# Products of zeros behind three steps of the first triangular solve, and two transposes tied to their written place

## The chip, the core and the metric

The kernel runs on one core of a Trainium2 chip. The metric is the device time of one execution in microseconds (us); the time before is the median of three runs. The engines are called PE (TensorE; its weight loads are listed apart, as PEld), DVE (VectorE), ACT (ScalarE), POOL (GpSimd) and SP (SyncE, whose queue issues the loads and stores).

## The reference

Two parts follow each other. The first is a linear attention with the delta rule over 4 batches x 8 heads, 768 steps and head size 48, in f32; the second is one wide layer on its result, with 3072 tokens, 384 inputs and 2048 hidden columns.

```python
k_n = k / (np.linalg.norm(k, axis=-1, keepdims=True) + 1e-06)
for t in range(S):
    y[:, :, t] = q_t @ state
    v_old = k_t @ state
    state = state + beta_t * outer(k_t, v_t - v_old)
h = x @ w_in
g = h * tanh(log1p(exp(h)))
out = g @ w_out
```

## The kernel before

**Stages.** The 768 steps are cut into 12 chunks of 64, and every two chunks form a group. Inside a chunk the steps depend on each other through a triangular system, so the kernel inverts triangles first. `early(g)` (line 253) does it for a group: DVE transposes the keys of each of the two chunks (`kt`, line 264), PE forms the products of keys with keys (`pg`, line 283), DVE takes the masked part (`d`, line 286), transposes it (`gt`, line 294), scales it, and then solves by forward substitution. A step j of the solve is two DVE instructions, a multiply into the tile `pr` (line 336) and an addition into `gt` (line 338). For the first two groups the triangles are cut into halves of 16 rows, so that j runs from 1 to 14; `merge` puts the halves together with small PE products (`ma`, line 375, and `mb`, line 386). The tile `pr` has one buffer: each step's `pr` takes the place of the one before. Behind the last step DVE scales the result and transposes it twice (`tt`, line 345, and `tu`, line 349); `ma` reads `tu`.

After that a chunk goes through `s_a`, `s_b`, `s_gq`, `s_z` and `s_y` (small products, all recorded under line 433, told apart by their tiles `ta`, `tb`, `gq`, `pz`, `py` and `ps`), and its 256 rows of results are transposed (`xt`) for the wide layer. `moe(n)` does that layer for a chunk: `g1(fp)` forms `h` (line 575) and a chain of ACT and DVE steps from it (lines 588 to 595, of which 589, 593 and 595 are DVE's), `g2(fp)` sums into `acc` (line 610).

**Conversions.** The weights come as 64-bit floats. `convert` (line 206) turns 28 parts of them, one by one, into two f32r halves: one ACT step (line 219), four DVE steps (lines 221 to 227), a product with the identity (`loi` or `loo`, line 238, f32, and line 241), and two ACT copies. They are laid between the other work over about the first 160 us.

**Order of work.** Every piece of work is a generator that is put on a plan with times (`put`); `run` pops them in order of planned time, and `defer` puts a follow-up a little later. Plan times are the author's estimates, not device time. `us(t)` turns a position in chunks into a plan time: `us(0)` is 76, `us(1)` is 140. What is popped is written into the program in that order. Up to plan time 90 the framework orders all engines anew, by a simulated timeline with the written order as priority, and may let an instruction whose inputs seem ready float ahead; from 90 on PE keeps the order in which it was written, and the other engines are still ordered by the framework. `order(a, b)` and `tc.keep_in_program_order(a)` add an edge without a wait: `a` stays behind `b`, or behind the instruction of the same engine that was written last before it. For groups from the third on the transposes of the keys are already tied in this way (line 267). For the second group they are written at plan times 85 and 92.

**Loads.** The keys of chunks 2 and 3 have source tiles of their own, loaded early; SP's queue issues all loads in a chain (`load`, line 169).

**Products of zeros.** `keep_warm(n)` (line 631) issues n bf16 products of 128 x 128 zeros with 128 x 512 zeros into the tile `warm`, 14 + 3 + 6 of them near the start of the plan.

Of the kernel before, what the change touches and what calls it, by code (L numbers as in the profile page):

```python
# [35 lines left out]
def kernel(  # L36
# [22 lines left out]
    nc = tc.nc  # L59


    TN = dict(fg=2, pl=range(0, 28), po=8, pg=(), db=1, fixed=((90.,()),(1e9,('PE',))),
              d0=["k0",1,"k1","b",3,"q",3,"v","x",4,"k2",4,"k3",13],
              us=[76., 140., 192., 242.],
              warm=[(0.5,14),(16.5,3),(18.,6)],
# [3 lines left out]
              cv=[(10.5,0),(12.8,1),(16,1.6),(23,2),(36,3),(74,13),(120,27.2),(123,28)],  # L69
              e1=[85,86,87.2,92,93,94.2,107,111], s1=(0.62,0.98), f1=0.985, m2=(1.0,1.02,1.03,1.05), m3=(1.18,1.2,1.22,1.24),  # L70
              prep1=52., prep2=0.4, c0=0.12, ab=(0.04,0.08), c1=(0.3,0.45,0.68,0.82), c2=(0.2,0.38,0.57,0.75), cc=(0.05,0.28,0.5,0.72),
              u1g=(1.085,1.12,1.45,1.3), ug=(0.81,0.93,1.56), g2=(-3.2,-2.75,-2.7,-2.69,-2.67,-2.64,-2.631), gg=(-4.05,-3.85,-3.692,-3.691,-2.85,-2.692,-2.691), tx=1.1, sg=-1.5, clk=1e9, mg=(-1.39, -1.36, -1.33, -1.30))
    FG = TN['fg']
    B, H, S, D = q.shape
    NT, DM = out.shape
# [1 line left out]
    P = 128  # L77
# [88 lines left out]

    loaded = []

    def load(dst, src):

        m = nc.sync.dma_start(out=dst, in_=src)  # L171
        if loaded and len(loaded) < TN.get('lo', 150):
            order(m, loaded[-1])
        loaded.append(m)

    def load_src(dst, src, n):
        for hh in range(2):
            for ch in range(2):
                w = 32 if ch == 0 else D - 32
                for tb in range(2):  # L180
                    t0 = C * n + 32 * tb
                    r0 = 64 * (1 - hh) + 32 * ch
                    load(dst[r0:r0 + 32, :, tb, :w], src[hh, t0:t0 + 32, :, 32 * ch:32 * ch + w])


    def load_w(parts):
# [66 lines left out]
    def early(g):  # L253
        dt = ap.tile([P, 2, NP, 32], F32, tag="d", name=f"d{g}", bufs=TN["db"])
        split = g < FG
        dts[g] = dt
        for t2 in range(2):
            n = 2 * g + t2
            ks = srcs.get((g, t2), ksrc)
            if g > 1 and t2 == 0:  # L260
                load_src(ks, kk, n)
                yield
            kt = kts[n] = ap.tile([P, NP, 2, 32], F32, tag="kt", name=f"kt{n}", bufs=3)
            m = nc.vector.transpose(kt.rearrange("p a b c -> p (a b c)"), ks.rearrange("p a b c -> p (a b c)"))
            m
            if g > 1:
                tc.keep_in_program_order(m)
                if t2 == 0:
                    load_src(ks, kk, n + 1)
            yield  # L270
            at = ats[n] = ap.tile([P, NP, 32], F32, tag="at", name=f"at{n}", bufs=3)
            for h8 in range(2):
                tensor(1.05)
                ps = pa.tile([P, 8, C], F32, tag="at", name=f"pg{n}_{h8}")
                for p8 in range(8):
                    p = 8 * h8 + p8

                    for c in range(2):
                        for hh in range(2):
                            r = slice(64 - 64 * hh, 128 - 64 * hh)  # L280
                            r0 = 64 * hh + 32 * c
                            mv = kt[r, p] if c else kt[r, p, 0:1, :].broadcast_to([64, 2, 32])
                            nc.tensor.matmul(ps[r0:r0 + 32, p8, :], kt[r, p, c, :], mv, start=True, stop=True)

                def out(t2=t2, ps=ps, at=at, pr=slice(8 * h8, 8 * h8 + 8)):
                    nc.vector.tensor_tensor(out=dt[:, t2, pr, :], in0=ps[:, :, 32:],
                                            in1=bcast_mid(lmask, 8), op=ALU.mult)
                    nc.scalar.copy(out=at[:, pr, :], in_=ps[:, :, 0:32])

                defer(1.2, out)  # L290
                yield
        gr = ap.tile([P, 33, 32], F32, tag="gt", name=f"gt{g}", bufs=1)
        gt = gr[:, :32]
        nc.vector.transpose(gt, dt.rearrange("p a b f -> p f (a b)"))
        gf = gt.rearrange("p a b -> p (a b)")
        if split:

            nc.gpsimd.memset(gt[:, 16:, 0:16], 0.0)
            nc.gpsimd.memset(dt[:, :, :, 0:16], 0.0)

        ss = ap.tile([P, 32], F32, tag="ss", name=f"ss{g}", bufs=1)
        nc.vector.tensor_scalar(ss, gf[:, ::33], 1e-30, None, op0=ALU.max)
        y = ap.tile([P, 32], F32, tag="y", name=f"y{g}", bufs=1)
        nc.scalar.activation(y, ss, AF.Ln, scale=0.25)
        nc.scalar.activation(y, y, AF.Exp, scale=0.5)
        yield
        rc = ap.tile([P, 32], F32, tag="rc", name=f"rc{g}", bufs=1)
        nc.vector.reciprocal(rc, y)
        nc.vector.scalar_tensor_tensor(ss, ss, 0.25, rc, op0=ALU.mult, op1=ALU.mult)
        nc.vector.scalar_tensor_tensor(ss, ss, 1e-6, y, op0=ALU.add, op1=ALU.add)  # L310
        nc.vector.reciprocal(rc, ss)
        nb = ap.tile([P, 32], F32, tag="nb", name=f"nb{g}", bufs=1)
        nc.vector.scalar_tensor_tensor(nb, rc, -1.0, rc, op0=ALU.mult, op1=ALU.mult)
        nc.vector.tensor_tensor(out=nb, in0=nb, in1=betaT[:, g, :], op=ALU.mult)

        nb_, sz = (2, 16) if split else (1, 32)
        blk = gr.rearrange("p a b -> p (a b)")[:, :nb_ * (1056 // 2)] if split else gf
        blk = blk.rearrange("p (x r) -> p x r", x=nb_)[:, :, :32 * sz].rearrange("p x (i j) -> p x i j", j=32)
        blk = blk[:, :, :, :sz]
        by_col = [P, nb_, sz, sz]  # L320
        nc.vector.tensor_tensor(
            out=blk, in0=blk, in1=nb.rearrange("p (x j) -> p x j", x=nb_).unsqueeze(2).broadcast_to(by_col),
            op=ALU.mult)
        nc.gpsimd.memset(gf[:, ::33], 1.0)
        bp = ap.tile([P, 32], F32, tag="bp", name=f"bp{g}")
        nc.vector.tensor_scalar(bp, nb, -1.0, None, op0=ALU.mult)
        ne = nes[g] = ap.tile([P, 32], F32, tag="ne", name=f"ne{g}")
        nc.vector.transpose(ne, ss)  # L328
        yield
        for j in range(1, sz - 1):  # L330
            m = sz - 1 - j
            pr = ap.tile([P, 512], F32, tag="prod", name=f"pr{g}_{j}", bufs=1)
            pv = pr[:, :nb_ * m * j].rearrange("p (x a b) -> p x a b", x=nb_, b=j)
            below, xj = blk[:, :, j + 1:, :j], blk[:, :, j:j + 1, :j].broadcast_to([P, nb_, m, j])
            nj = blk[:, :, j + 1:, j:j + 1].broadcast_to([P, nb_, m, j])
            nc.vector.tensor_tensor(out=pv, in0=nj, in1=xj, op=ALU.mult)  # L336
            yield
            nc.vector.tensor_tensor(out=below, in0=below, in1=pv, op=ALU.add)  # L338
            yield
        nc.vector.tensor_tensor(  # L340
            out=blk, in0=blk, in1=bp.rearrange("p (x i) -> p x i", x=nb_).unsqueeze(3).broadcast_to(by_col),
            op=ALU.mult)
        if not split:
            yield
        nc.vector.transpose(tt2[:, :, :, 32:].rearrange("p a b i -> p i (a b)"), gt)
        tn = tns[g] = ap.tile([P, 2, NP, 32], F32, tag="tn", name=f"tn{g}", bufs=1)
        if split:
            tu = tus[g] = ap.tile([P, 2, NP, 16], F32, tag="prod", name=f"tu{g}", bufs=1)
            nc.vector.transpose(tu.rearrange("p a b j -> p j (a b)"),
                                      gt[:, :, 0:16].rearrange("p i j -> p j i"))  # L350
            ym = yms[g] = ap.tile([P, 33, 32], F32, tag="gt", name=f"ym{g}", bufs=1)
            nc.gpsimd.memset(ym[:, :32, 16:], 0.0)
        else:
            nc.vector.transpose(tn.rearrange("p a b j -> p j (a b)"), gt.rearrange("p i j -> p j i"))
            for t2 in range(2):
                move_diagonal(t2)
        yield
# [270 lines left out]
    zb = zero.bitcast(BF16)  # L628
    warm = ph.tile([P, 512], F32, tag="h", name="warm")

    def keep_warm(n):
        tensor(0.4 * n)
        for _ in range(n):
            nc.tensor.matmul(warm, zb[:, 0:P], zb[:, :512], start=True, stop=True)

    ys, xs = {}, {}

# [22 lines left out]
    def load_beta():  # L660
        for c in range(2):
            for hh in range(2):
                for t2 in range(2):
                    r0 = 64 * hh + 32 * c + 16 * t2
                    load(betaT[r0:r0 + 16], bt[hh, c, t2])

    todo = list(parts)

    def loads(order):
        for x in order:  # L670
# [11 lines left out]
                    load_k(0, h)  # L682
            else:
                m = int(x[1])
                load_src(srcs[m // 2, m % 2], kk, m)

    took = {s_a: 1.2, s_b: 1.2, s_gq: 1.1, s_z: 1.1, s_y: 1.9}

# [35 lines left out]
    for i, p in enumerate(parts):  # L724
        ts = [when(i + j / 4 + 0.1) for j in range(4)]
        end = ts[3] + 0.75
        put(convert(*p), ts[0] - 0.75, *ts, end, end + 0.8, end + 1.4, end + 2.4)

    units = [moe(n) for n in range(NS)]
    todo1 = [(n, fp) for n in range(NS) for fp in range(NFP)]  # L730
# [89 lines left out]
```

## Time and profile before

| | |
|---|---|
| time, median of 3 runs | 704.14 us (702.71 to 704.75) |
| the profiled execution, its own time | 702.13 us |
| its span, first to last instruction | 700.3 us |
| granted clock, mean | 0.944 |
| PE busy | 633.6 us, 90% of the span |
| DVE busy | 478.4 us, 68% |
| ACT busy | 440.0 us, 63% |
| the key transposes of chunks 2 and 3 (line 264) | start at 45.26 and 76.11 us, 1.25 us each |
| first `ma` behind the first solve | 58.58 us |

A row of the order of time reads: start, duration (of the first to the last, where several are merged), engine, line, operation, written tile <- read tiles, shape, count, and in brackets how long the engine had been idle before it and what ended that. "issue" there means that nothing in the profile explains the wait. A row of a table by stretches gives for each engine its busy time and number of instructions, then the granted PE clock as a share of full speed, the mean busy share of the DMA engines, and GB/s.

### The profile page before, as it was taken

How to read it: one execution, taken by the hardware profiler on the slowest of the kernel's cores; microseconds unless marked ns; L12 is line 12 of the kernel's file. 1: busy time of each engine (PE TensorE's matmuls, PEld its weight loads, DVE VectorE, ACT ScalarE, POOL GpSimd, SP SyncE). 2: the span in 40 equal slices, each digit the busy share in tenths (PEclk: the TensorE clock that was granted, in tenths of full speed). 3: DMA queues.
4: the chain of work that ended last, by engine and by line, in shares of the span. 5: the costliest groups of instructions: out<-in, count | busy, mean ns of one | idle time of the engine just before them, and what ended most of it. 6: DMA issues, size and time to landing. Idle time of an engine off the chain costs nothing.

```text
span 700.3 us, 23223 instructions
## 1 busy us (share of the span) xinstructions
PE 633.6 (90%) x10163; PEld 582.5 (83%) x10163; DVE 478.4 (68%) x1048; ACT 440.0 (63%) x821; POOL 48.8 (7%) x84
## 2 busy tenths in 40 slices
PE   6543899889979899999999999999999999999993
PEld 3313777679879799999999999999999999999993
DVE  4794278996449975589974799856899645443440
ACT  1350368776535766856758766668566687777771
POOL 5000000101000001010010000010100100000000
PEclk9575589999989999999999999999999999999998
DMA  5999230113131232222212312321121111000000
GB/s 81 223 244 348 40 61 12 22 15 59 27 63 26 42 59 39 41 52 35 46 37 42 63 25 39 66 37 30 31 35 47 28 21 36 13 22 3 12 12 24
DMA packets 160214, 37.79 MB, mean 54 GB/s; under 512 B 153456, under 2 KB 156528, under 8 KB 160112
## 3 DMA queue, kind: packets, MB, share of 16 engines
q1 hardware_dynamic: 160112, 36.30, 25.4%
q8 instruction: 80, 1.31, 0.7%
q14 instruction: 22, 0.18, 0.1%
HBM read 31.56 MB, written 4.72 MB: 52 GB/s over the span
## 4 chain that ended last, share of the span: by engine, by line
PE 44%; DVE 26%; ACT 13%; SPq 7%; issue 6%; DMA 3%; DVEq 0%; ACTq 0%
PE h L575 15%; PE acc L610 15%; SPq L171 7%; DVE e L593 4%; PE gq L433 3%; ACT e L591 3%; DVE g L595 3%; DVE pr L336 3%; DVE gt L338 3%; ACT e L590 2%; PE py L433 2%; ACT e L592 2%; DVE e L589 2%; DVE xx L480 2%; DVE xx L421 2%
## 5 line engine op out<-in xcount | busy, mean ns | idle before, releaser
L575 PE MATMUL h<-x,wi 128*128 128x256 f32 x1728 | 227.0, 285 | 4.3 <-DVE e L593 3.6
L575 PEld LDWEIGHTS h<-x,wi 128*128 128x128 f32 x1728 | 214.4, 188 | 10.5 <-DVE e L593 2.9
L610 PE MATMUL acc<-wo,g 128*128 128x384 f32 x1152 | 221.1, 341 | 0.0
L610 PEld LDWEIGHTS acc<-wo,g 128*128 128x128 f32 x1152 | 198.4, 188 | 3.2
L593 DVE SCALAR_TENSOR_TENSOR e<-e,h 128x512 f32<-128x512 f32 x96 | 65.8, 685 | 97.1 <-ACT e L592 93.8
L590 ACT ACTIVATE e<-e 128x512 f32<-128x512 f32 x96 | 60.6, 631 | 74.6 <-DVE e L589 74.1
L594 ACT CAST g<-e 128x512 fp32r<-128x512 f32 x96 | 59.5, 619 | 41.3 <-DVE e L593 40.8
L595 DVE TENSOR_TENSOR g<-e,g 128x512 fp32r<-128x512 f32 x96 | 65.1, 678 | 20.6 <-ACT g L594 19.4
L588 ACT ACTIVATE e<-h 128x512 f32<-128x512 f32 x96 | 57.1, 595 | 28.5 <-PE h L575 27.6
L591 ACT ACTIVATE e<-e 128x512 f32<-128x512 f32 x96 | 60.5, 631 | 2.6
L592 ACT ACTIVATE e<-e 128x512 f32<-128x512 f32 x96 | 60.6, 632 | 2.4
L589 DVE TENSOR_SCALAR e<-e 128x512 f32<-128x512 f32 x96 | 40.8, 425 | 25.1 <-ACT e L588 24.8
L338 DVE TENSOR_TENSOR gt<-gt,pr 128x84 f32<-128x84 f32 (+14 forms) x148 | 46.0, 311 | 3.2
L336 DVE TENSOR_TENSOR pr<-gt 128x84 f32<-128x84 f32 (+14 forms) x148 | 45.9, 310 | 2.5
L433 PE MATMUL gq<-xx,kt 64*64 64x112 f32 (+1 forms) x768 | 44.6, 264 | 0.9 <-ACT wo L243 0.9
L433 PEld LDWEIGHTS py<-xx 128*64 128x64 f32 x768 | 38.8, 142 | 6.3 <-issue 3.2
L480 DVE TENSOR_TENSOR xx<-gq,amask 64x256 f32<-64x256 f32 x96 | 40.2, 418 | 5.4 <-PE gq L433 4.7
L433 PE MATMUL py<-xx 128*64 128x48 f32 x768 | 42.8, 229 | 0.0
L433 PEld LDWEIGHTS gq<-xx,kt 64*64 64x64 f32 x768 | 38.2, 140 | 2.6 <-issue 1.3
L414 POOL TENSOR_TENSOR vt<-vt,ne 128x384 f32<-128x384 f32 x24 | 21.0, 880 | 277.8 <-DVE ne L328 123.3
L433 PE MATMUL pz<-vt,tt 64*64 64x48 f32 x768 | 38.0, 235 | 2.4 <-ACT tt L462 1.3
L433 PEld LDWEIGHTS pz<-vt,tt 64*64 64x64 f32 x768 | 34.4, 139 | 6.3 <-ACT tt L462 2.8
(112 smaller groups left out, 718.0 us busy)
## 6 DMA issues: line engine op xcount, KB each, us to landing
ri<-in_moe_w_in_dram SPq DMA_DIRECT2D x12, 512.0 KB
ro<-in_moe_w_out_dram SPq DMA_DIRECT2D x16, 384.0 KB
vt<-in_v_dram SPq DMA_DIRECT2D x48, 96.0 KB
xx<-in_k_dram SPq DMA_DIRECT2D x48, 96.0 KB
out_dram<-o SPq DMA_DIRECT2D x24, 192.0 KB
qsrc<-in_q_dram SPq DMA_DIRECT2D x48, 64.0 KB
ksrc<-in_k_dram SPq DMA_DIRECT2D x44, 64.0 KB
qsrc<-in_q_dram SPq DMA_DIRECT2D x48, 32.0 KB
```

The costliest lines, as they stand in the source:

```text
L336: nc.vector.tensor_tensor(out=pv, in0=nj, in1=xj, op=ALU.mult)
L338: nc.vector.tensor_tensor(out=below, in0=below, in1=pv, op=ALU.add)
L433: last[:] = [nc.tensor.matmul(*a, start=True, stop=True)]
L575: nc.tensor.matmul(h[:, f2, :], wt["i", f * P // WI * NCH + c][:, i2, f0:f0 + P], x[:, c, :], start=(i == 0), stop=(i == 3 * NCH - 1))
L588: for d, f in ((0.7, lambda: nc.scalar.activation(e, h, AF.Exp, scale=-1.0)), (0.55, lambda: nc.vector.tensor_scalar(e, e, EXP20, 1.0, op0 ...
L590: (0.65, lambda: nc.scalar.activation(e, e, AF.Square)),
L591: (0.65, lambda: nc.scalar.activation(e, e, AF.Ln, bias=0.5, scale=0.5)),
L592: (0.7, lambda: nc.scalar.activation(e, e, AF.Exp, scale=-1.0)),
L593: (0.8, lambda: nc.vector.scalar_tensor_tensor(e, e, -1.0, h, op0=ALU.add, op1=ALU.mult)),
L594: (0.7, lambda: nc.scalar.copy(out=gg[:, 0], in_=e)),
L595: (0.8, lambda: eng.tensor_tensor(out=gg[:, 1], in0=e, in1=gg[:, 0], op=ALU.subtract))):
L610: nc.tensor.matmul(acc[t], gg[:, a, f2, ts_], wt["o", f][:, i2, :], start=(f == 0 and i == 0), stop=(f == NF - 1 and i == 2))
```

## The change

Group 0 alone is touched by the first part: behind the multiply of steps 4, 8 and 12 one f32 product of zeros with 64 columns of that step's `pr` is written, and behind it, kept in order, 5, 6 and 8 bf16 products of zeros. The second part ties the two key transposes of group 1 to their written place. The rest of the diff gives functions arguments that stay at their defaults (`queue`, `pd`, `sc`), takes an estimate out of `keep_warm` and writes the limit 150 in place of a lookup with the same default.

```diff
-    TN = dict(fg=2, pl=range(0, 28), ...
+    TN = dict(fg=2, sc=(), ws={4: 5, 8: 6, 12: 8}, pl=range(0, 28), ...
...
             m = nc.vector.transpose(kt.rearrange("p a b c -> p (a b c)"), ks.rearrange("p a b c -> p (a b c)"))
-            m
+            if g > 0:
+                tc.keep_in_program_order(m)
             if g > 1:
-                tc.keep_in_program_order(m)
                 if t2 == 0:
                     load_src(ks, kk, n + 1)
...
             nc.vector.tensor_tensor(out=pv, in0=nj, in1=xj, op=ALU.mult)
+            if g == 0 and j in TN['ws']:
+
+                keep_warm(TN['ws'][j], nc.tensor.matmul(warm[:, :64], zero[:, 0:P], pr[:, 0:64], start=True, stop=True))
             yield
...
-    def keep_warm(n):
-        tensor(0.4 * n)
+    def keep_warm(n, after=None):
         for _ in range(n):
-            nc.tensor.matmul(warm, zb[:, 0:P], zb[:, :512], start=True, stop=True)
+            m = nc.tensor.matmul(warm, zb[:, 0:P], zb[:, :512], start=True, stop=True)
+            if after is not None:
+                order(m, after)
+                after = m
```

More of the change, by code (lines that the diff above doesn't have):

```diff
@@ L59 @@
     nc = tc.nc
-    TN = dict(fg=2, pl=range(0, 28), po=8, pg=(), db=1, fixed=((90.,()),(1e9,('PE',))),
+    TN = dict(fg=2, sc=(), ws={4: 5, 8: 6, 12: 8}, pl=range(0, 28), po=8, pg=(), db=1, fixed=((90.,()),(1e9,('PE',))),
               d0=["k0",1,"k1","b",3,"q",3,"v","x",4,"k2",4,"k3",13],
@@ L71 @@
               prep1=52., prep2=0.4, c0=0.12, ab=(0.04,0.08), c1=(0.3,0.45,0.68,0.82), c2=(0.2,0.38,0.57,0.75), cc=(0.05,0.28,0.5,0.72),
-              u1g=(1.085,1.12,1.45,1.3), ug=(0.81,0.93,1.56), g2=(-3.2,-2.75,-2.7,-2.69,-2.67,-2.64,-2.631), gg=(-4.05,-3.85,-3.692,-3.691,-2.85,-2.692,-2.691), tx=1.1, sg=-1.5, clk=1e9, mg=(-1.39, -1.36, -1.33, -1.30))
+              u1g=(1.085,1.12,1.45,1.3), ug=(0.81,0.93,1.56), g2=(-3.2,-2.75,-2.7,-2.69,-2.67,-2.64,-2.631), gg=(-4.05,-3.85,-3.692,-3.691,-2.85,-2.692,-2.691), tx=1.1, sg=-1.5, pd={}, clk=1e9, mg=(-1.39, -1.36, -1.33, -1.30))
     FG = TN['fg']
@@ L167, with load, load_src @@
     loaded = []
-    def load(dst, src):
+    def load(dst, src, queue=None):
+        if queue is not None:
+            m = queue.dma_start(out=dst, in_=src)
+            if by_scalar:
+                order(m, by_scalar[-1])
+            by_scalar.append(m)
+            return
         m = nc.sync.dma_start(out=dst, in_=src)
-        if loaded and len(loaded) < TN.get('lo', 150):
+        if loaded and len(loaded) < 150:
             order(m, loaded[-1])
         loaded.append(m)
-    def load_src(dst, src, n):
+    by_scalar = []
+    def load_src(dst, src, n, queue=None):
         for hh in range(2):
@@ L182, in load_src @@
                     r0 = 64 * (1 - hh) + 32 * ch
-                    load(dst[r0:r0 + 32, :, tb, :w], src[hh, t0:t0 + 32, :, 32 * ch:32 * ch + w])
+                    load(dst[r0:r0 + 32, :, tb, :w], src[hh, t0:t0 + 32, :, 32 * ch:32 * ch + w], queue)
     def load_w(parts):
@@ L664, in load_beta @@
                     r0 = 64 * hh + 32 * c + 16 * t2
-                    load(betaT[r0:r0 + 16], bt[hh, c, t2])
+                    load(betaT[r0:r0 + 16], bt[hh, c, t2], nc.scalar if "b" in TN['sc'] else None)
     todo = list(parts)
@@ L684, in loads @@
                 m = int(x[1])
-                load_src(srcs[m // 2, m % 2], kk, m)
+                load_src(srcs[m // 2, m % 2], kk, m, nc.scalar if x in TN['sc'] else None)
     took = {s_a: 1.2, s_b: 1.2, s_gq: 1.1, s_z: 1.1, s_y: 1.9}
@@ L726 @@
         end = ts[3] + 0.75
-        put(convert(*p), ts[0] - 0.75, *ts, end, end + 0.8, end + 1.4, end + 2.4)
+        put(convert(*p), ts[0] - 0.75, *ts, *(end + TN['pd'].get(i, 0.0) + d for d in (0.0, 0.8, 1.4, 2.4)))
     units = [moe(n) for n in range(NS)]
```

## The prediction

> **What bounds the kernel now.** I read the page first, then the busy time by stretches, then the order of time from 41 to 119 us.
>
> ```profile
> span 700.3 us, 23223 instructions
> PE 633.6 (90%) x10163; PEld 582.5 (83%) x10163; DVE 478.4 (68%) x1048; ACT 440.0 (63%) x821; POOL 48.8 (7%) x84
> q8 instruction: 80, 1.31, 0.7%
> ...
> PE 44%; DVE 26%; ACT 13%; SPq 7%; issue 6%; DMA 3%; DVEq 0%; ACTq 0%
> ```
> ```profile
> 50.00:58.50 8.50, 0.00 (x0) 0.00 (x0) 7.82 (x21) 0.69 (x2) 0.00 (x0) 0.50 0.88 217
> 61.20:65.40 4.20, 0.00 (x0) 0.00 (x0) 0.00 (x0) 0.00 (x0) 0.00 (x0) 0.50 1.03 416
> 109.20:145.40 36.20, 30.19 (x546) 23.72 (x539) 35.23 (x89) 26.76 (x56) 3.45 (x5) 1.00 0.13 19
> 190.00:690.00 500.00, 490.25 (x7232) 469.74 (x7230) 346.05 (x742) 342.74 (x626) 25.02 (x38) 0.99 0.20 36
> ```
>
> Columns of the second: stretch, length, busy us (and instructions) of PE, PEld, DVE, ACT, POOL, granted clock, DMA share, GB/s. From 190 us on PE is 98% busy, and nothing of the change lies there: a time won or lost before 145 us shifts all the rest. In the head three things set the pace in turn: DVE alone while the first solve ends (50 to 58.5, PE idle at clock 0.50), nothing at all from 61.2 to 65.4, and DVE again from 109 to 145 (35.23 busy of 36.20 us, while PE has 6 us to spare). So a microsecond of DVE counts in the first and the third stretch; PE's idle time in the first is free.
>
> **The change, part by part.** The unused hooks (second queue, `pd`, `lo`) are off with the values given, and `tensor()` only moves a clock that is read above plan time 1e9. Two parts are left: the products, and the order kept for the key transposes of the second group, which the diff carries too (`g > 0` in place of `g > 1`).
>
> *A. The third key transpose (chunk 2) leaves the first solve.*
>
> ```profile
> 41.39 0.24 DVE L336 TENSOR_TENSOR pr<-gt 128x88 f32<-128x88 f32 x1
> ...
> 43.92 0.25 DVE L336 TENSOR_TENSOR pr<-gt 128x100 f32<-128x100 f32 x1
> ...
> 45.26 1.25 DVE L264 STREAM_TRANSPOSE kt<-ksrc 128x1024 f32<-128x1024 f32 x1 [0.48 <-issue]
> ...
> 51.03 0.27 DVE L336 TENSOR_TENSOR pr<-gt 128x112 f32<-128x112 f32 x1
> ...
> 51.65 0.27 DVE L336 TENSOR_TENSOR pr<-gt 128x108 f32<-128x108 f32 x1
> ...
> 53.42 0.23 DVE L336 TENSOR_TENSOR pr<-gt 128x72 f32<-128x72 f32 x1
> ...
> 53.95 0.21 DVE L336 TENSOR_TENSOR pr<-gt 128x52 f32<-128x52 f32 x1
> ...
> 57.45 0.99 DVE L349 STREAM_TRANSPOSE tu<-gt 128x512 f32<-128x512 f32 x1
> ```
>
> Nothing needs it before 112 us, yet it stands between steps 5 and 6: DVE waits 0.48 us and works 1.25 us. Gone from there, all behind it comes 0.48 + 1.25 = 1.73 us sooner. Bounds: -1.73, and 0 if what stands behind was itself late. I take **-1.73**, since DVE was busy without a gap behind it.
>
> *B. Three steps wait for a product.* Steps 4, 8 and 12 (88, 112 and 72 columns in the rows above) each give PE one f32 product of 64 columns that reads `pr`; `pr` has one buffer, so step 5, 9 or 13 may not write it until that product has read it. Behind it stand 5, 6 and 8 bf16 products of 512 columns.
>
> ```profile
> 2.70:7.10 4.40, 4.40 (x11) 1.64 (x12) 0.22 (x1) 0.00 (x0) 4.25 (x6) 1.00 0.80 100
> 7.40:9.50 2.10, 2.10 (x11) 0.96 (x10) 2.03 (x5) 0.00 (x0) 1.88 (x8) 1.00 1.07 233
> ```
> ```profile
> 32.71 2.08 PE L238 MATMUL loi<-spare,ident 128*128 128x512 f32 x2 [2.38 <-DVE spare L227]
> 43.72 1.12 PE L238 MATMUL loi<-mi,ident 128*128 128x512 f32 x2 [1.19 <-DVE mi L227]
> ```
>
> The kernel's 23 products of zeros fill 2.7 to 9.8 us: 4.40/11 = 0.40 us each at first, 2.10/11 = 0.19 later. (The clock column shows 1.00 in both; the halving shows that the first were slow.) One f32 product of 512 columns takes 2.08 us at half clock and 1.12 at full: if the part that goes by columns halves, it is 1.92 and the fixed part 0.16. For 64 columns that makes 0.40 us slow, 0.28 fast. A handover costs about 0.14 us (`tu` ends at 58.44, the first `ma` starts at 58.58, quoted under C). At step 4, 2.3 us of conversions lie before step 5, which hides it: 0. At step 8 the multiply ends at 51.30; 0.14 + 0.40 + 0.14 makes 51.98 for step 9 in place of 51.65: +0.33. Step 12's product stands behind six slow ones: 51.84 + 6 x 0.40 = 54.24, + 0.40 + 0.14 = 54.78 in place of 53.95: **+0.83** in all. At full clock both waits are +0.21 and +0.26, 0.47 in all. I take 0.83, as the clock is 0.50 in that stretch. The last eight end at 54.64 + 8 x 0.40 = 57.84, before `tu` does at 58.44 + 0.83, so they delay no `ma`.
>
> *C. PE's program gets longer in front of two stalls.*
>
> ```profile
> 58.58 1.90 PE L375 MATMUL ma<-tu,d 16*32 16x16 f32 x128 [13.51 <-DVE tu L349]
> ...
> 65.45 1.36 PE L386 MATMUL mb<-tt,ym 32*32 32x16 f32 x83 [4.33 <-issue]
> ...
> 66.73 1.97 PE L433 MATMUL gq<-xx,kt 64*64 64x64 f32 x32
> ...
> 68.64 0.57 PE L433 MATMUL ta<-tt,at 32*32 32x32 f32 x13
> ...
> 71.64 1.59 PE L433 MATMUL ta<-tt,at 32*32 32x32 f32 x51 [2.43 <-issue]
> ```
>
> PE stops twice with nothing to wait for. Between the stops lie 83 + 32 + 13 = 128 products with their weight loads, 256 instructions; the page shows 80 packets of instructions for PE's 20326, 254 each. So I read the stops as the next block of program arriving late while the DMA share is 1.03. The new products are 3 x 2 (an f32 one counts twice, as L238's "x2") + 19 = 25 pairs, so each stop comes 25 pairs earlier in the work: the first ends 25 x 1.90/128 = 0.37 us sooner, the next 6.2 us after it as now, and behind the second stand 25 pairs more, 11 of `gq` (11 x 1.97/32 = 0.68) and 14 of `ta` (14 x 1.59/51 = 0.44). Net **+0.74**. Bounds: -0.37 if only the first half holds, +0.74.
>
> The Trainium skill (Runtime: NRT & Kernel Launch, Instruction fetch mechanics) says that program comes in 16 KiB blocks of 256 instructions and that crossing into one is mostly hidden. The block size agrees with the 128 pairs, the hiding does not: 4.33 and 2.43 us stand open here. With it hidden this term would be 0 and the sum 0.74 lower.
>
> *D. The clock.* 19 products against PE's idle stretch can raise the clock before `ma`. But `ma` at 14.8 ns a product is at the pace of its issue, and what it wins is taken by the stop at 61.2, which ends by its own latency. 0 in the forecast; the other reading is a rival.
>
> *E. Two transposes move into the stretch that DVE bounds.* The call ties a transpose behind the DVE instruction written just before it. The first is written at plan time 85; the last DVE work before is the masking of `s_gq(1, 0)` (at 76 + 64 x 0.12 + 1.2 = 84.88). The second is written at 92, behind line 593 of the second `g1` (at 86 + 5.65 = 91.65).
>
> ```profile
> 76.11 1.25 DVE L264 STREAM_TRANSPOSE kt<-ksrc 128x1024 f32<-128x1024 f32 x1
> ...
> 109.50 0.85 DVE L480 TENSOR_TENSOR xx<-gq,amask 64x256 f32<-64x256 f32 x2
> ...
> 111.99 1.99 PE L283 MATMUL pg<-kt 64*32 64x64 f32 x128
> ...
> 115.98 0.68 DVE L593 SCALAR_TENSOR_TENSOR e<-e,h 128x512 f32<-128x512 f32 x1
> 116.02 1.10 PE L283 MATMUL pg<-kt 64*32 64x64 f32 x64
> ...
> 118.72 0.91 PE L238 MATMUL loo<-mo,ident 128*128 128x384 f32 x2 [1.60 <-ACT wi L243]
> ```
>
> So they go from 45 and 76 us to behind 110.35 and 116.66. The second leaves a DVE gap, which saves nothing. In 109.2 to 145.4 DVE has 36.20 - 35.23 = 0.97 us free; 2 x 1.25 = 2.50 more costs 2.50 - 0.97 = 1.53 if all of it can be used, 2.50 if none. PE says the same: chunk 3's `pg` can start at 116.66 + 1.25 + 1.25 + 0.14 = 119.30, 3.28 us late, of which PE now waits 1.60 anyway, so 1.68. I take **+1.53**, the nearest to both.
>
> **Sum.** -1.73 + 0.83 + 0.74 + 1.53 = +1.4 us (its bounds: -1.73 + 0.47 + 0 + 1.53 = +0.3, and 0 + 0.83 + 0.74 + 2.50 = +4.1). The profiled execution took 702.13 us (span 700.3 and 1.8 around it), so 703.5 like for like. The median of the runs is 704.14, 2 us above it, which gives 705.5. About 0.3%, 2.1 us, is what can be told from no change: the forecast is no measurable change.
>
> **The rivals.**
>
> *The clock lasts (faster).* If the products keep the clock full beyond `ma`, half-clock work up to 92 us speeds up.
>
> ```profile
> 75.07 1.92 PE L433 MATMUL tb<-at,tn 32*32 32x32 f32 x64
> ...
> 83.90 2.08 PE L238 MATMUL loi<-spare,ident 128*128 128x512 f32 x2
> ...
> 104.16 1.14 PE L433 MATMUL ta<-tt,at 32*32 32x32 f32 x60
> ...
> 108.67 1.19 PE L433 MATMUL tb<-at,tn 32*32 32x32 f32 x62
> ```
> ```profile
> 88.10:91.40 3.30, 3.23 (x64) 3.07 (x64) 0.50 0.02 5
> 93.20:95.20 2.00, 1.91 (x64) 1.79 (x64) 1.00 0.40 73
> ```
> ```profile
> 10.80:14.20 3.40, 1.25 (x92) 1.09 (x80) 2.52 (x4) 0.00 (x0) 0.00 (x0) 1.00 0.36 43
> 14.00:15.00 1.00, 0.00 (x0) 0.00 (x0) 1.00 (x3) 0.00 (x0) 0.00 (x0) 0.61 0.07 11
> ```
>
> `ta` would save 1.59 - 51 x 1.14/60 = 0.6, `tb` 0.7, the conversion 2.08 - 1.12 = 1.0, the 64 `py`/`ps` products 3.23 - 1.91 = 1.3: 3.6, and another 0.7 from a second conversion at 91 us by the same rows; -4.3 against +1.4 gives -2.9: 701.2. Against it: the stop from 61.2 to 65.4 stays, and the clock fell at 14.2 us after 2.2 us without a product.
>
> The Trainium skill (TensorE: Matmul & The Clock Gate, Part 1) has the rule behind this rival: about 3.4 us of sustained products free the clock, an idle window as long takes it away. By its second half the 4.2 us stop undoes what the first half gave; the fall at 14.2 agrees with a window that is mostly idle.
>
> *The moved transposes are hidden (no change).* If ACT and PE, not DVE, carry 109 to 145, E is 0 and the sum -0.2: 704.0. For it: PE and ACT stand in that part of the chain too. Against: 97% DVE.
>
> *PE's written order passes the wait on (slower).* From plan time 90 PE runs in the order written. If the wait of 1.60 us behind chunk 3's `pg` is for DVE work that is late as well, the two don't overlap, and E is the whole 3.28: -1.73 + 0.83 + 0.74 + 3.28 = +3.1, 707.3. It decides once the second transpose ends later than 116.02 and the wait for `wi` moves with it.
>
> **How the numbers follow.** Forecast 0.45 (same 0.30, slower 0.15, as its bounds reach +4.1); clock 0.20 (faster 0.15, same 0.05); hidden 0.18 (faster 0.05, same 0.12, slower 0.01); written order 0.17 (slower 0.14, same 0.03). Faster 0.20, same 0.50, slower 0.30. The range goes from the clock rival's 701.2, a little lower, to the upper bound of the sum, 708.2: 701.0 to 708.4.
>
> **What would show it.** A: no L264 between steps 5 and 6, `tu` about 0.9 us sooner (-1.73 + 0.83). B: gaps of 0.3 and 0.5 us before steps 9 and 13, ended by PE `warm`. C: the stops after some 20 `mb`, and after 21 `gq`. D: clock 0.50 again by 66 us. E: L264 behind 110 and 116 us, and `pg` of chunk 3 at 119. The prediction is wrong if the clock is full through 75 to 90 us, or if PE's first product after 145 us comes no later than before although E's transposes stand there.

## The result, and the profile after

The changed kernel takes 716.04 us (median of 6 runs, 711.11 to 718.19) against 704.22 us before: a ratio of 1.0163, with an interval of 1.0138 to 1.0188, or +11.5 us. The forecast was 705.5 us with a range up to 708.4, so the change costs eight times what the sum said, and the time lies outside the range. The profiled execution took 714.48 us.

The page of the changed kernel; the engines' rows give busy us, share of the span and instructions:

```profile
span 712.8 us, 23273 instructions
PE 639.9 (90%) x10188; PEld 585.8 (82%) x10188; DVE 480.3 (67%) x1048; ACT 440.1 (62%) x821; POOL 49.3 (7%) x84
q8 instruction: 80, 1.31, 0.7%
```

PE has 25 products and 25 weight loads more, as counted, and is busy 6.3 us longer; most of that is the added products themselves, which lie in time that PE had free (5.17 us from 50 to 58 us, below). The rest of the 12.5 us is idle time. To find the places I followed the same PE products through both executions (start after minus start before):

| product | before | after | difference |
|---|---|---|---|
| first `ma` of the first group | 58.58 | 58.12 | -0.46 |
| `ma` ahead of the second pair of stages | 168.29 | 171.66 | +3.37 |
| next `ma` | 180.71 | 187.79 | +7.08 |
| `h` of the wide layer | 325.66 | 333.48 | +7.82 |
| the `h` behind it | 330.64 | 340.22 | +9.58 |
| a later `h` | 520.54 | 532.13 | +11.59 |
| end of the span | 700.3 | 712.8 | +12.5 |

Only +3.4 us is there by 166 us, where the prediction had put the whole change: -0.5 up to the first `ma`, +1.0 over the two stops, +0.9 from 78 to 100 us (the clock comes back at 94.1 us in place of 92.7, and PE waits 0.43 us for ACT), and +1.9 where the two transposes now stand. Three quarters of the loss arise behind that, nearly all of it in places that the prediction had not looked at: 170 to 190 us, 325 to 345 us and 520 to 560 us.

The order of time of the changed kernel, first solve and the two stops:

```profile
50.00 0.69 PE L347 MATMUL warm<-pr,zero 128*128 128x64 f32 x2 [4.46 <-DVE pr L344]
...
50.72 0.27 DVE L344 TENSOR_TENSOR pr<-gt 128x108 f32<-128x108 f32 x1 [0.47 <-PE warm L347]
...
53.48 0.21 DVE L344 TENSOR_TENSOR pr<-gt 128x52 f32<-128x52 f32 x1 [0.48 <-PE warm L347]
...
58.12 1.28 PE L386 MATMUL ma<-tu,d 16*32 16x16 f32 x128 [2.95 <-DVE tu L360]
59.37 0.36 PE L397 MATMUL mb<-tt,ym 32*32 32x16 f32 x20
64.60 1.68 PE L397 MATMUL mb<-tt,ym 32*32 32x16 f32 x108 [4.87 <-issue]
66.21 1.33 PE L444 MATMUL gq<-xx,kt 64*64 64x64 f32 x20
71.07 0.90 PE L444 MATMUL gq<-xx,kt 64*64 64x64 f32 x12 [3.53 <-issue]
```

Steps 9 and 13 wait for the product of zeros, 0.47 and 0.48 us; no transpose of keys stands between the steps any more. `ma` runs at 1.28 us in place of 1.90. PE stops behind 20 `mb` and behind 20 `gq`: 25 and 25 pairs earlier in the work than before, and longer than before (4.87 and 3.53 against 4.33 and 2.43 us).

The clock over these stretches (third number from the end; the columns are those of the prediction), changed kernel:

```profile
50.00:58.00 8.00, 5.17 (x18) 2.41 (x18) 6.54 (x16) 0.37 (x1) 0.00 (x0) 0.80 0.88 200
58.00:75.00 17.00, 8.48 (x376) 8.06 (x378) 3.06 (x8) 1.66 (x4) 1.73 (x3) 0.56 0.88 301
75.00:109.00 34.00, 32.24 (x653) 25.43 (x649) 18.28 (x38) 18.09 (x39) 2.86 (x4) 0.72 0.30 49
```

It is full for part of the first (from 53.2 us) and the first 2 us of the second (to 60.0), and in the third no longer than before.

The two moved transposes and what waits for the second, changed kernel:

```profile
111.44 1.25 DVE L272 STREAM_TRANSPOSE kt<-ksrc 128x1024 f32<-128x1024 f32 x1
...
118.18 1.24 DVE L272 STREAM_TRANSPOSE kt<-ksrc 128x1024 f32<-128x1024 f32 x1
...
119.56 1.10 PE L291 MATMUL pg<-kt 64*32 64x64 f32 x64 [1.95 <-DVE kt L272]
```

**170 to 190 us.** PE in the order of time, first of the kernel before, then of the changed one, and between them what the DMA queues moved from 173.5 to 176 us in the changed one (packets, MB, share of 16 engines):

```profile
168.29 1.42 PE L375 MATMUL ma<-tu,d 16*32 16x16 f32 x128
169.60 0.89 PE L386 MATMUL mb<-tt,ym 32*32 32x16 f32 x64
170.43 2.40 PE L575 MATMUL h<-x,wi 128*128 128x256 f32 x18
```
```profile
q8 instruction: 1, 0.02, 2.4%
```
```profile
171.66 1.41 PE L386 MATMUL ma<-tu,d 16*32 16x16 f32 x128
172.97 0.84 PE L397 MATMUL mb<-tt,ym 32*32 32x16 f32 x64
173.74 0.39 PE L586 MATMUL h<-x,wi 128*128 128x256 f32 x1
176.43 3.63 PE L586 MATMUL h<-x,wi 128*128 128x256 f32 x17 [2.30 <-DVE tt L400]
```

The 18 `h` products run through before, and stop for 2.30 us behind the first after. The page names DVE's `tt` as the releaser, but `h` reads only `x` and `wi`. One packet of program is moved in that time. The place is that of a block's border, too: PE's recorded instructions (products, weight loads and semaphore waits), counted in order, leave the remainder 192 to 194 when divided by 256 at this stop, and so they do at all stops named "issue" of 0.3 us or more behind 60 us, in all 14 traces. The kernel before has smaller stops of this kind behind 166 us as well: 1.07 us at 184 and 0.33 us at 204. Behind the stop the clock is half: 17 products take 3.63 us where 18 took 2.40.

**325 to 345 us.** The wide layer's steps on DVE before the loss, first of the kernel before, then of the changed one, each followed by PE's waits there and near 530 us:

```profile
314.87 0.27 DVE L338 TENSOR_TENSOR gt<-gt,pr 128x108 f32<-128x108 f32 x1
315.06 0.42 DVE L589 TENSOR_SCALAR e<-e 128x512 f32<-128x512 f32 x1
315.40 0.28 DVE L336 TENSOR_TENSOR pr<-gt 128x130 f32<-128x130 f32 x1
...
330.64 2.65 PE L575 MATMUL h<-x,wi 128*128 128x256 f32 x18 [0.50 <-DVE e L593]
...
520.54 2.66 PE L575 MATMUL h<-x,wi 128*128 128x256 f32 x18 [0.55 <-DVE e L593]
```
```profile
322.68 0.27 DVE L349 TENSOR_TENSOR gt<-gt,pr 128x108 f32<-128x108 f32 x1
322.99 0.29 DVE L344 TENSOR_TENSOR pr<-gt 128x130 f32<-128x130 f32 x1
323.32 0.30 DVE L349 TENSOR_TENSOR gt<-gt,pr 128x130 f32<-128x130 f32 x1
323.65 0.32 DVE L344 TENSOR_TENSOR pr<-gt 128x150 f32<-128x150 f32 x1
324.00 0.32 DVE L349 TENSOR_TENSOR gt<-gt,pr 128x150 f32<-128x150 f32 x1
324.23 0.42 DVE L600 TENSOR_SCALAR e<-e 128x512 f32<-128x512 f32 x1
...
340.22 3.77 PE L586 MATMUL h<-x,wi 128*128 128x256 f32 x18 [2.26 <-DVE e L604]
...
532.13 2.40 PE L586 MATMUL h<-x,wi 128*128 128x256 f32 x18 [2.26 <-DVE e L604]
```

The work is the same, its order isn't: four more DVE instructions, two steps of a later solve (`pr` and `gt` with 130 and 150 columns, 1.24 us), stand ahead of the `e` step, and the chain behind it ends 2.26 us too late for `h` in place of 0.50. The clock falls there too, but not at the like wait near 530 us, where the 18 `h` take 2.40 us. The instruction lists of the two programs say the same: PE's, SP's and POOL's orders are equal but for the added products, while DVE's differs not only where the transposes moved (positions 74 to 178 of 1048) but also at 322 to 325, 509 to 597 and 837 to 933, and ACT's (821) at 57 to 103 and 221 to 606.

Two later stretches, first before, then after:

```profile
109.00:146.00 37.00, 30.91 (x561) 24.22 (x553) 35.83 (x91) 27.48 (x57) 3.45 (x5) 1.00 0.12 18
...
320.00:345.00 25.00, 24.49 (x300) 23.32 (x296) 24.11 (x58) 17.60 (x33) 0.83 (x1) 1.00 0.30 44
```
```profile
109.00:146.00 37.00, 32.02 (x579) 25.35 (x578) 34.64 (x82) 27.11 (x56) 3.45 (x5) 0.95 0.12 18
...
320.00:345.00 25.00, 22.74 (x257) 21.87 (x252) 23.38 (x60) 15.63 (x29) 0.90 (x1) 0.93 0.17 25
```

The clock is below 1.00 in both, where before it was full.

### The profile page after: what moved, and what is told of

Same layout as the page of the kernel before. It is cut to its first block, busy times and chain, and to the rows that moved or that the text cites. A ratio compares the mean times of both kernels' runs of the same rounds, so it can differ in the third digit from the quotient of the medians.

```text
span 712.8 us, 23273 instructions
## 1 busy us (share of the span) xinstructions
PE 639.9 (90%) x10188; PEld 585.8 (82%) x10188; DVE 480.3 (67%) x1048; ACT 440.1 (62%) x821; POOL 49.3 (7%) x84
## 3 DMA queue, kind: packets, MB, share of 16 engines
q8 instruction: 80, 1.31, 0.7%
## 4 chain that ended last, share of the span: by engine, by line
PE 52%; DVE 27%; ACT 9%; issue 5%; SPq 3%; DMA 2%; DVEq 0%
PE h L586 19%; PE acc L621 17%; SPq L177 3%; PE gq L444 3%; DVE e L604 3%; DVE pr L344 3%; PE py L444 3%; DVE g L606 2%; DVE gt L349 2%; ACT e L602 2%; DVE xx L432 2%; DVE xx L491 2%; ACT e L601 2%; ACT e L603 2%; DVE e L600 2%
## 5 line engine op out<-in xcount | busy, mean ns | idle before, releaser
L586 PE MATMUL h<-x,wi 128*128 128x256 f32 x1728 | 230.7, 288 | 9.7 <-DVE e L604 6.8
L586 PEld LDWEIGHTS h<-x,wi 128*128 128x128 f32 x1728 | 217.9, 192 | 16.1 <-DVE e L604 7.4
```

The source lines that it names most:

```text
L586: nc.tensor.matmul(h[:, f2, :], wt["i", f * P // WI * NCH + c][:, i2, f0:f0 + P], x[:, c, :], start=(i == 0), stop=(i == 3 * NCH - 1))
```

## The experiments

**Theory.** Two things that the prediction left out make the loss. The first: 25 more pairs move *every* later border between blocks of PE's program by 50 instructions, and behind 170 us some borders fall where PE is too fast for the next block. The second: the framework planned DVE and ACT anew far behind the change. **Rivals:** the moved transposes carry the late losses; or the products cost by themselves, by their waits or the clock.

Since the framework plans anew after any edit, the orders were written out in all kernels but the changed one itself: each instruction of DVE, ACT and PE is tied behind the one before it in a given list, without a wait. Edits of these lists are shown in words below.

```diff
+    for engine, order_ in ORDERS.items():
+        traced = [i for i in nc.cur_bb.bb.instructions if str(i.engine).split('.')[-1] == engine and type(i).__name__ not in QUIET]
+        for x, y in zip(order_, order_[1:]):
+            tc.add_manual_dep(traced[y], traced[x].name,
+                              mybir.DependencyInfo(mybir.DependencyClass.NoSync, mybir.DependencyReason.DATA),
+                              reason="written order")
```

All kernels compute the whole reference. The differences below are (ratio - 1) x 704 us against the kernel before on the same chip, with the interval of the ratio. Writing the orders out costs nothing that shows: two kernels that have it stand at -1.1 and -0.1.

| kernel | median, us | difference, us |
|---|---|---|
| products alone | 710.38 | +6.1 (3.7 to 8.5) |
| transposes alone | 703.47 | -0.5 (-1.8 to 0.8) |
| later order alone | 706.90 | +3.7 (1.9 to 5.5) |
| 25 tiny pairs | 709.11 | +5.2 (3.4 to 7.0) |
| 128 tiny pairs | 703.32 | -1.1 (-2.1 to -0.1) |
| changed, borders put back | 709.61 | +5.6 (3.9 to 7.3) |
| changed, later order put back | 709.13 | +6.2 (4.0 to 8.3) |
| changed, both put back | 706.52 | +1.5 (0.1 to 2.9) |
| one transpose behind `tu` | 701.26 | -2.3 (-3.5 to -1.1) |
| 50 tiny pairs | 711.76 | +6.8 (4.3 to 9.2) |
| changed, once more | 713.95 | +10.0 (8.2 to 11.8) |
| products, borders put back | 704.17 | -0.1 (-1.3 to 1.0) |

### Products alone

```diff
-    TN = dict(fg=2, pl=range(0, 28), ...
+    TN = dict(fg=2, sc=(), ws={4: 5, 8: 6, 12: 8}, pl=range(0, 28), ...
...
+            if g == 0 and j in TN['ws']:
+                keep_warm(TN['ws'][j], nc.tensor.matmul(warm[:, :64], zero[:, 0:P], pr[:, 0:64], start=True, stop=True))
```

> Kernel before with the products of zeros of the change alone: both key transposes stay at their old places, and DVE and ACT keep the order of before, written out as an order without waits. Theory (block stop): the 25 more pairs of PE's program carry a border between two blocks of program into the fast products at 170 to 176 us, where PE then stops 2.3 us and loses the clock for 3.4 us. With B (+0.83) and C (+0.74, measured in the changed kernel nearer to +1.1) that makes 0.83 + 1.1 + 3.7 = about +5.6 us, with a PE stop of some 2.3 us near 174. Rival (new plan): the loss behind 164 us comes from the new order of DVE and ACT or from the moved transposes; then +0.83 + 1.1 = +1.6 to +1.9 us, and no stop at 174.

Measured +6.1 us. Behind 250 us only 0.3 us more is lost, and PE stops in the stretch named (1.42 us in place of the 2.3 expected, behind three `h`, with 3.57 us for the other 15). The rival that lays the late loss on the orders or the transposes alone falls for this stretch.

### Transposes alone

```diff
-DVE: ... kt2 inside step 5 ... kt3 at 76 us ...
+DVE: ... xx of s_gq(1, 0), kt2 ... e (line 593) of the second g1, kt3 ...
```

> Kernel before with the two key transposes alone at the places they have in the changed kernel, no products of zeros, all else in the order of before. Theory: A -1.73 and E between +1.53 and +2.50, so 0 to +0.8 us, all of it there by 145 us and nothing more behind it. Rival (written order): E is 3.28, +1.5 us. Rival (the transposes are behind the late losses too): +5 us or more, in steps at 330 and 530 us as in the changed kernel.

Measured -0.5 us (-1.8 to 0.8): within the theory's reach, against +5, and there are no late waits. Followed as above, PE is 1.4 us early at 78 us and 0.45 us late from 119 us on: E is 1.9 us. The written-order rival asked for +1.5, which the interval leaves out. E at 0 would have given -1.7, at the edge of the interval; it is the trace that rules it out.

### Later order alone

```diff
-    DVE: order_before          ACT: order_before
+    DVE: order_before[:250] + order_after[250:]    ACT: order_before[:210] + order_after[210:]
```

> Kernel before up to DVE's instruction 250 and ACT's 210 (about 170 us); from there on DVE and ACT follow the order that the changed kernel has. No products of zeros, no moved transposes. Theory (new plan): the later order alone makes PE wait for a DVE step at about 330 us (+2.9) and at 520 to 553 us (+2.5), less 0.8 at 383: +4.5 us. Rival (the waits come only because the changed kernel gets there late or with another clock): 0 within 1 us.

Measured +3.7 us, and PE waits where the changed kernel does:

```profile
335.46 3.84 PE L577 MATMUL h<-x,wi 128*128 128x256 f32 x18 [2.27 <-DVE e L595]
...
527.45 2.40 PE L577 MATMUL h<-x,wi 128*128 128x256 f32 x18 [2.26 <-DVE e L595]
```

Not one product or transpose is added here. The order alone makes these waits; which of the instructions that changed places makes each of them was not tried. The clock falls behind the first of the two waits and not behind the second.

### 25 tiny pairs, and 128

```diff
             nc.vector.tensor_tensor(out=pv, in0=nj, in1=xj, op=ALU.mult)
+            if g == 0 and j == 8:
+                for _ in range(25):   # 128 in the second kernel, 50 in a third
+                    nc.tensor.matmul(warm[0:32, 0:16], zb[0:32, 0:32], zb[0:32, 0:16], start=True, stop=True)
```

> Kernel before, all orders as before, and 25 tiny products of 32 x 32 zeros with 32 x 16 zeros in PE's idle time ahead of the first ma: nothing waits for them, but PE's program is 50 instructions longer from there on, as in the changed kernel. Theory (block stop): C at +0.7 to +1.1, then the stop of 2.3 us near 174 with the fall of the clock behind it, +3.7: about +4.7 us in all. Rival (the 25 pairs matter only at the two stops at 61 and 69 us): +0.7 to +1.1. Rival (the stops are not those of program blocks): 0.

> Kernel before, all orders as before, with 128 tiny products of zeros (as in the run with 25, five times as many) in PE's idle time ahead of the first ma. 128 pairs are one whole block of program, so every border between blocks falls on the same product as before. Theory (block borders): the place of the borders is what costs, so 0 within 1 us, the stops at the same products as before (behind 45 mb, behind 13 ta) and none near 174. Rival (the products themselves, or a longer program as such): at least the +5.2 us of the run with 25.

25 pairs cost 5.2 us, and five times as many cost nothing (-1.1). This is the cleanest pair of the study. PE with 25, and then with 128:

```profile
172.12 0.50 PE L580 MATMUL h<-x,wi 128*128 128x256 f32 x2
174.38 2.05 PE L580 MATMUL h<-x,wi 128*128 128x256 f32 x16 [1.75 <-issue]
```
```profile
62.59 0.84 PE L391 MATMUL mb<-tt,ym 32*32 32x16 f32 x45
67.10 1.35 PE L391 MATMUL mb<-tt,ym 32*32 32x16 f32 x83 [3.67 <-issue]
...
73.30 1.59 PE L438 MATMUL ta<-tt,at 32*32 32x32 f32 x51 [2.44 <-issue]
...
172.51 3.67 PE L580 MATMUL h<-x,wi 128*128 128x256 f32 x18
```

With 25, `h` stops as in the changed kernel, and here the page says "issue". The fall of the clock that was expected behind this stop did not come in this execution (16 `h` in 2.05 us). It is also one of the quicker ones: it took 706.23 us where the median is 709.11, and of its 4.2 us over the profile before 2.3 are there at the first `ma`, ahead of the first stop. So the 5.2 us rest on the medians, and the trace shows where and not how much. With 128 the first two stops are back behind 45 `mb` and 13 `ta`, and all 18 `h` run without a stop. (They run at half clock here, so a fall of the clock in this stretch does not need the stop.) So it is the place of the border that costs, not the number of products.

### 50 tiny pairs

> Kernel before with 50 tiny products of zeros ahead of the first ma in PE's idle time. By hand from the two stops alone: the first border falls ahead of ma, the next two 81 pairs later in the work than before, worth 1.3 us, so -1.3. By a block model (no block of 256 instructions is passed in less than about 3.65 us, as blocks 19 and 20 show in the kernel before with 3.74 and 3.61, or 6.2 us while the loads run; the borders of all 80 blocks moved by 100 instructions over PE's times in the kernel before): +4.9 us, with stops near 173, 187 and 199 us. For 25 pairs the same model gives +7.7 where +5.2 was measured, so +3 to +5 here.

Measured +6.8 us: the reckoning by the first two stops alone has the wrong sign, the block model the right one, about 2 us too low. Of the three stops that it named, one stands near 173 us and one near 200 us (1.71 us); none stands near 187. The first, 25 pairs earlier than with 25 tiny pairs:

```profile
171.29 1.41 PE L380 MATMUL ma<-tu,d 16*32 16x16 f32 x128
172.60 0.63 PE L391 MATMUL mb<-tt,ym 32*32 32x16 f32 x41
175.86 0.51 PE L391 MATMUL mb<-tt,ym 32*32 32x16 f32 x23 [2.62 <-issue]
```

With 25 the stop came behind 64 `mb` and 2 `h`, here behind 41 `mb`: 25 pairs between them. The least time for a block that the model takes, 3.65 us, does not hold everywhere (see the last section). Whether another place of the borders is better than that of the kernel before was not tried.

### The changed kernel with its parts put back

```diff
+            if g == 0 and j == 8:
+                for _ in range(103):
+                    nc.tensor.matmul(warm[0:32, 0:16], zb[0:32, 0:32], zb[0:32, 0:16], start=True, stop=True)
```

> The changed kernel, its orders written out, with 103 tiny products of zeros more in PE's idle time ahead of the product of step 8: 25 + 103 = 128 pairs, so the borders fall where they fell before. Theory (block borders): what the 25 pairs cost alone, 5.2 us, goes, so +11.8 - 5.2 = +6 to +7 us over the kernel before, no stop at 174, waits for DVE at about 335 and 527 as in the changed kernel. Rival (the borders do not add to the rest, or the stop at 174 has its own cause in the changed kernel): +10 to +12.

```diff
-    DVE: order_after           ACT: order_after
+    DVE: order_after[:250] + order_before[250:]    ACT: order_after[:210] + order_before[210:]
```

> The changed kernel, but from DVE's instruction 250 and ACT's 210 on these two follow the order of before. Theory (the parts add up): products alone (+6.5) and transposes alone (-0.4) are left, so about +6 to +7 us over the kernel before, with the stop near 174 and no waits for DVE at 338 and 530. Rival (the later order costs the changed kernel nothing of its own): still +11 to +12.

Both edits together:

> The changed kernel with both: 103 tiny products for the borders and the later order of before. What is left of the change are its three waits in the first solve, the products and the two moved transposes. Theory (parts add up): 6.5 - 5.2 - 0.4 = about +1 us over the kernel before; by the terms of the prediction without C: -1.73 + 0.83 + 1.53 to 1.9 = +0.6 to +1.0. Rival (something else in the changed kernel costs too): +3 us or more.

And the changed kernel itself, beside the kernel before on the chip of these last runs:

> The changed kernel itself once more, on the chip of these runs, for the sum of the parts: moved transposes -0.4, products with the border at its old place about +1.9, the border +5, the later order +3 to +3.5, together +9.5 to +10; first measured +11.8. If the parts add up and the rest is scatter between sets of runs: +9 to +11. If the parts make each other dearer: +11.5 to +12.5 again.

Measured +5.6, +6.2, +1.5 and +10.0. Putting the borders back wins 10.0 - 5.6 = 4.4 without the old order and 6.2 - 1.5 = 4.7 with it. Putting the order back wins 3.8 (10.0 - 6.2) or 4.1 (5.6 - 1.5). With both put back 1.5 us are left. Each part is worth much the same with the other and without it, so the parts add up: 1.5 + 4.6 + 3.9 = 10.0. Each of these differences of two rows is good to some 2 to 3 us. The changed kernel's first measurement was +11.5 (9.7 to 13.2), which overlaps with 10.0; where the 1.5 us between the two come from is open. With the old order the stop near 174 is there, and PE no longer waits 2.3 us for DVE at 338 and 530:

```profile
174.81 3.99 PE L588 MATMUL h<-x,wi 128*128 128x256 f32 x17 [2.13 <-issue]
```

### Products with the borders put back

The products alone as above, and the 103 tiny pairs.

> Kernel before with the products of zeros of the change and 103 tiny ones more, so that the borders of program blocks lie as before; both key transposes at their old places, DVE and ACT in the order of before. What is left is B, the three DVE steps that wait for a product. Theory: +0.83 by the prediction, +0.94 to +1.07 by the waits in the changed kernel (0.47 + 0.48) and in the run with the products alone (0.47 + 0.60). Rival (the products cost more than the waits that the profile names, for example by the clock that they raise and lose again): +1.9 us, the difference of the run with both parts undone (+1.5) and of the transposes alone (-0.4).

Measured -0.1 us (-1.3 to 1.0). The waits are there:

```profile
52.88 0.27 DVE L346 TENSOR_TENSOR pr<-gt 128x108 f32<-128x108 f32 x1 [0.47 <-PE warm L352]
...
55.77 0.21 DVE L346 TENSOR_TENSOR pr<-gt 128x52 f32<-128x52 f32 x1 [0.60 <-PE warm L352]
```

The rival of +1.9 falls. The theory's +0.83 to +1.07 lies at the upper edge of the interval: the runs neither show it nor rule out most of it. With the products alone at +6.1, the border is worth 6.2 us here; the four estimates of it are 4.4, 4.7, 5.2 and 6.2.

### One transpose behind tu

```diff
-DVE: ... multiply of step 5, kt2, addition of step 5 ... tt, tu, ...
+DVE: ... multiply of step 5, addition of step 5 ... tt, tu, kt2, ...
```

> Kernel before with one transpose moved: chunk 2's key transpose goes from its place between steps 5 and 6 of the first solve to just behind tu, where DVE has nothing to do from 58.4 to 66.0 us; chunk 3's stays, and there are no products of zeros. Theory: A without E, -1.73 by the profile of before and up to -3.3 where the transpose had waited 2.06 us for its keys (as in the run with 25 products), so -1.7 to -2.5 us, and E by the difference to the run with both transposes moved (-0.4): +1.3 to +2.1. Rival (what is won in the solve is lost at PE's two stops at 61 and 70 us, which end by their own latency): 0 to -0.5.

```profile
56.84 1.00 DVE L351 STREAM_TRANSPOSE tu<-gt 128x512 f32<-128x512 f32 x1
57.72 1.20 DVE L266 STREAM_TRANSPOSE kt<-ksrc 128x1024 f32<-128x1024 f32 x1
```

Measured -2.3 us (-3.5 to -1.1): A's gain without E, and a version that beats both kernels, if by 0.3% only. The transpose lies in time that DVE had free, waits for nothing, and is not in the stretch that DVE bounds. Against the kernel with both transposes moved (-0.5) E comes to +1.8, give or take 1.8 by the two intervals.

## Why the prediction was wrong

**The step that failed** stands in its first part: that from 190 us on "nothing of the change lies there: a time won or lost before 145 us shifts all the rest". Two things of the change lie behind 145 us.

- *The borders (term C).* The prediction read the stops rightly as program that comes late, in blocks of 128 pairs, and placed the first to the pair and the second one pair off (behind 21 `gq`; between 20 `gq` and the old place behind 13 `ta` lie 12 + 13 = 25 pairs, not 11 + 14). It then priced the shift at these two stops only, +0.74, with -0.37 and +0.74 as bounds. But a program that grows by 25 pairs between 42 and 54 us has all its later borders elsewhere too, and 170 to 200 us is a stretch of fast small products like the first. The same term, with all borders in it, measures 4.4 to 6.2 us. This is the term that was mis-sized, and the larger half of the miss. At the two stops themselves little can be read: they last 3.5 to 4.9 and 2.2 to 3.5 us from one execution to the next (that with 50 pairs left out), and from the first `ma` to 78 us PE lost between -0.5 and +1.0 us in the five traces with 25 pairs more.
- *The planning (not in the sum at all).* The text before the prediction said that from plan time 90 on only PE keeps the written order and that the others are "still ordered by the framework"; the prediction used that for the two transposes and for nothing else. Planned anew, four steps of a solve pass a step of the wide layer near 323 us, and PE waits 2.26 us at 338 and 530 us, where it waited about half a microsecond. 3.7 to 4.1 us.

The other terms:

- **A, right.** -1.73 forecast; alone, behind `tu`, -2.3 (-3.5 to -1.1). The transpose stood inside step 5, between its multiply (43.92 us) and its addition (46.73 us), not behind it, which changes nothing in the sum. The 0.48 us that the page calls "issue" is read as the transpose's wait for its keys: in four of the seven executions with it at the old place the page names their load. It varies: see the last section. With B, `tu` came 0.48 us sooner and not 0.9, but the solve as a whole ran 0.45 us later by then (the addition of step 3 at 41.36 us in place of 40.91).
- **B, right in the trace.** +0.33 and +0.50 forecast, waits of 0.47 and 0.48 measured, and nothing at step 5. In the time of the kernel -0.1 (-1.3 to 1.0).
- **D, right in what it comes to, wrong in a reason.** The clock was full from 53.2 us and half again at 60.0, and the stop from 59.7 to 64.6 us took what `ma` won. But `ma` at 14.8 ns a product was not at the pace of its issue: at full clock it took 1.28 us for 128, 10.0 ns. The rival in which the clock lasts fell.
- **E, right in size.** +1.53 forecast with 2.50 as upper bound, 1.8 to 1.9 measured. The transposes came 1.1 and 1.5 us later than said, as the whole stretch did. The rivals that hide it or make it 3.28 both fell by the trace (PE's 1.9 us); the interval of the medians alone leaves out 3.28 and just reaches 0. Not foreseen: PE's wait there costs the clock (0.95 in that stretch after, 1.00 before).
- A, B and E together were +0.63; with borders and later order put back the changed kernel stands at +1.5 (0.1 to 2.9). That part of the forecast lies within the interval.

The Trainium skill (Runtime: NRT & Kernel Launch, Instruction fetch mechanics), which the prediction weighed, says that crossing into a new block is mostly hidden. The trace of the changed kernel disagrees at six places (4.87, 3.53, 2.30, 0.42, 0.77 and 0.64 us); over most of the 80 blocks it agrees.

**The range** failed for the same reason: its upper end was made of bounds for the terms named, and the missing ones had no bound. A side that says "all the rest only shifts" needs a reason for each engine, and there was one for PE's order alone. Neither of the two signs that the prediction had named for being wrong came: the clock was not full through 75 to 90 us, and PE's first product behind 145 us came later than before. It failed where it had named no sign.

**Still open.** Why the clock falls at 173 us without a stop in the execution with 128 tiny pairs; and how much of B is left behind the two stops, which is below what these runs can tell.

## What to carry to other kernels

In a long unrolled program, instructions added anywhere move every later block border. Count where the borders fall before and after, or fill up to a whole block (25 pairs cost 5 us here, 128 cost nothing that shows). Compare the instruction lists of every engine before a change is priced, and hold the orders fixed when a part is to be measured: otherwise the planner's new order is measured with it. And ask of a transfer or a transpose not only what it delays, but whether the engine has free time a few microseconds on: moving one transpose 12 us later won 2.3 us.

## What the runs showed of the hardware

- **PE can stop at the border of a block of 256 instructions, until the next one has come.** Between the first two stops lie 128 pairs: 71.64 - 65.45 = 6.19 us before, 71.07 - 64.60 = 6.47 after, 73.30 - 67.10 = 6.20 with 128 tiny pairs, and 5.65 to 6.75 over all 14 traces. Near 174 us the same count of instructions ahead of the stop begins within `ma`: 62 `ma`, 64 `mb` and 2 `h` with 25 tiny pairs, 63, 64 and 1 in the changed kernel, 87 `ma` and 41 `mb` with 50. From there to the end of the stop it is 3.74, 4.16 and 4.22 us. The DMA engines are busier at the first stops (share 0.95 from 58.5 to 71.6 us before) than near 174 (0.46 from 173 to 176 us after); that this makes the difference was not tried.
- **This is no least time for every block.** PE ran through a block in 1.31 us at 290 us (50 tiny pairs) and in 2.28 us at 87 us (changed kernel) without a stop behind it. With 50 pairs the page shows two packets of program in the block ahead (281.5 to 290.2 us) and none in this one, so that the next block seems to have been there already. This is read from the traces and was not tried. Why the block was not there at the first stop, though PE had stood idle for 13.5 us ahead of `ma` in the kernel before, is open.
- **A wait that the page puts down to an engine can be such a stop.** The 2.30 us in the changed kernel were named "DVE tt"; the same stop was "issue" in the kernel with 25 tiny pairs, and in a second execution of the changed kernel itself (2.43 us).
- **The first transpose's wait for its keys varies.** In seven executions with it at the old place it was 0.39 to 2.06 us, 1.15 in the mean. The longest:

```profile
47.54 1.25 DVE L266 STREAM_TRANSPOSE kt<-ksrc 128x1024 f32<-128x1024 f32 x1 [2.06 <-DMA ksrc<-in_k_dram]
```

This wait lies on the path of the first solve, so it can be one source of the scatter of the kernel before (700.3 to 707.8 us over all runs on these chips). With the 1.25 us of the transpose the mean makes 2.4 us, nearer to the 2.3 measured for A than the 1.73 of one execution.
- **Short waits of PE can cost the clock too, but need not.** Behind a wait of 2.26 and 2.27 us the 18 `h` products took 3.77 us (changed kernel) and 3.84 us (later order alone) where 2.40 is usual: about 1.4 us more for one wait. Behind the second such wait of the same two executions, 2.26 us each, they took 2.40. Over the four traces that have these waits the clock fell behind four of eight.
